# The sink columns of the probabilities: their high and low parts moved from VectorE to ScalarE and GpSimd

## The chip, the core and the metric

The kernel runs on one core of a Trainium2 chip. A core has TensorE (matrix products and transposes, into PSUM), VectorE, ScalarE and GpSimd (elementwise work; GpSimd has no way to PSUM in this kernel, all its operands are in SBUF), and queues that issue DMA transfers. Each engine works through its own instructions in order and waits for the others by semaphores. The metric is the device time of one execution in microseconds (us); lower is better.

## What is computed

Three parts follow each other: attention with a few sink columns and a sliding window, a mixture of experts with one expert for each token, and a second mixture in which all experts are used, weighted by a matrix that is normalized by rows and columns in turn. The change lies in the first part:

```python
B, H, S, D = q.shape                      # 2, 8, 768, 64; n_sink = 4, window = 128
scores = scale * np.matmul(q, k.transpose(0, 1, 3, 2))
keep = (pos[None, :] < n_sink) | ((rel >= 0) & (rel < window))   # rel = row - column
scores = np.where(keep, scores, -1e9)
a = np.exp(scores - scores.max(-1, keepdims=True))
a = a / (a.sum(-1, keepdims=True) + 1e-9)
return np.matmul(a, v)
```

## The kernel before

**Tiling.** Attention goes over 8 groups, each a pair of heads of one batch element, and in each group over 6 units t = 0 to 5 of 128 rows; 48 units in all. A row of unit t needs the 128 columns of its own tile, the 128 of the tile before and, from t = 2 on, the 4 sink columns, which lie apart from them. So a score tile is 128 x 260: the tile before, 4 sink columns, its own tile (128 x 128 for t = 0).

**A unit.** `st_a` makes one head's scores: a product on TensorE (L359), mask and minimum on VectorE (L360, from PSUM), the exponential on ScalarE (L362), giving `pt` in SBUF. The product with v is made in float16 in two parts, high and low. `st_b` transposes `pt` on TensorE (L370, `tq`), ScalarE makes the high part `ph` from it (L388), VectorE the low part `pl` (L398). The sink columns go another way. `psk_hi` (L378) writes their high part, scaled by 16384, twice into `psk`; `psk_lo` (L382) writes the low part behind it. `st_b3` transposes `psk` (24 columns: three parts, two heads, four sinks) in one step on TensorE (L393, `tk`), and ScalarE copies it (L395, `skT`). `st_c` multiplies with v: the sink part first (L410, against `vk`), then the rest (L416 to L419, against `vs`). `norm` divides by the row sums for two units at a time (L427 to L432). There are 32 units with t of 2 or more, so 32 of each of L378, L382, L393 and L395.

**The next group's operands** (`prep`) are spread over eight steps: the transposes of k and q (L236, copied out by L239, L246, L248), the largest |v| (L254 to L277), and on GpSimd the scaling of v (L284, in the fifth step of a group), its low part (L287, twice) and the sink values `vk` (L297 to L302, a chain of six small instructions in the second step of the next group).

**Order.** In step i the loop (L484 to L535) works on four units: scores of unit i + 2, `psk` of unit i + 1, transposes of unit i, product of unit i - 1. Inside the loop the order of ScalarE's and of GpSimd's instructions is the program's own (`manual_schedule`, L482); TensorE's and VectorE's order is set by a planner at build time, near the program's. `psk_hi` is called early in a step, ahead of `st_b2` (ScalarE's L388), and `psk_lo` between the two `st_a`. `pt` has four buffers, `psk` three, `tq`, `sc` and `tp` two.

**Beside it.** Routing (`route`, L779) is spread over the steps from the fifth group on: logits on TensorE, small VectorE instructions, then the scatter of the rows of the first batch element by GpSimd (L750, then L751, an indirect DMA whose descriptors GpSimd makes). Near the end, from step 43 (`SPLIT0`), the first expert's weights are split: high parts on ScalarE (L775), low parts on GpSimd for the first two and on VectorE for the others (L776); after each pair the next weights are loaded into the freed buffers.

Of the kernel before, what the change touches and what calls it, by code (L numbers as in the profile page):

```python
# [8 lines left out]
F32 = mybir.dt.float32  # L9
# [5 lines left out]
AF = mybir.ActivationFunctionType  # L15
ALU = mybir.AluOpType
# [4 lines left out]
P = 128  # L21
# [5 lines left out]
G = 2  # L27
NS = 4
# [9 lines left out]
PSC = 16384.0  # L38
# [121 lines left out]
def attention_fast(nc, tc, c, a, x_bs, hooks):  # L160
# [6 lines left out]
    wk = st.enter_context(tc.tile_pool(name="af_wk", bufs=3))  # L167
# [206 lines left out]
    def psk_hi(u):  # L374
        if u and u.t >= 2:
            u.psk = wk.tile([P, 3, G, NS], F16, name="psk")
            u.pk = u.pt[:, :, P:SB]
            nc.vector.tensor_scalar(u.psk[:, 0:2], u.pk.unsqueeze(1).broadcast_to([P, 2, G, NS]), PSC, None, ALU.mult)  # L378

    def psk_lo(u):  # L380
        if u and u.t >= 2:
            nc.vector.scalar_tensor_tensor(u.psk[:, 2], u.pk, PSC, u.psk[:, 0], ALU.mult, ALU.subtract)  # L382

    def v3(u, x):
        return x[:, :, 1, :] if u.t == 0 else x.rearrange("p h c q -> p (h c q)")
# [57 lines left out]
    for gi, (b, g) in enumerate(groups):  # L443
        for t in range(NT):
            u = Ctx()
# [31 lines left out]
    head_masks()  # L477
    r.v_s()
    psk_hi(units[0])
    psk_lo(units[0])  # L480
    ms.close()
    st.enter_context(tc.manual_schedule(engines={ENG.Activation, ENG.Pool}))  # L482
    ready = []
    for i in range(len(units) + 2):  # L484
# [10 lines left out]
        steps.run("act", *ready)  # L495
        norm(un, 0)
        psk_hi(up)
        norm(un, 1)
        run(m0)
# [17 lines left out]
        if ua:  # L517
            st_a(ua, 0)
        psk_lo(up)
        run(m1)  # L520
        steps.run("dve")
# [1150 lines left out]
```

## Time and profile before

| | |
|---|---|
| median of 3 runs | 1324.7 us (1322.53 to 1326.58) |
| profiled execution, in all | 1326.13 us |
| its span, first to last instruction | 1324.3 us |
| TensorE busy | 1272.4 us (96%) |
| VectorE busy | 969.9 us (73%) |
| ScalarE busy | 578.7 us (44%) |
| GpSimd busy | 449.3 us (34%) |
| mean granted TensorE clock | 0.986 |

The page of the profile shows one execution. Engines: PE is TensorE's products, PEld its weight loads, DVE VectorE, ACT ScalarE, POOL GpSimd, SP the queue that issues DMA transfers. L360 is line 360 of the kernel. Busy time counts the time from an instruction's start to its end, and the records of neighbours can overlap. Idle time before an instruction is put down to what came last, as `<-DVE psk L382`. The granted clock is the share of full speed that TensorE was given: 1.00 is 2.4 GHz, 0.50 is 1.2 GHz. Times of one instruction in a list of groups are means in ns. A row in order of time gives the start and the length in us; in the list by stage, a row gives the stretch, its length, and how long each engine was busy in it.

### The profile page before, as it was taken

The page shows a single profiled execution, that of the slowest core. Times are in us where ns is not written, and L with a number is a line of the kernel's source. Part 1 is how long each engine was busy: PE and PEld are TensorE (multiplying, and loading weights), DVE is VectorE, ACT ScalarE, POOL GpSimd, SP SyncE. Part 2 cuts the span into 40 slices and gives each one's busy share as a digit, 9 for nine tenths or more (in the row PEclk, how much of TensorE's full clock was granted, in tenths as well). Part 3 has the DMA queues.
Part 4 walks back from the last instruction along what each step waited for, and adds up shares of the span by engine and source line. Part 5 has one row for each costly group of instructions (what it writes and reads, how often), then busy time and mean ns, then how long its engine had stood idle before and what let it go on. Part 6 is the DMA issues. An engine that isn't in the chain of part 4 may idle for free.

```text
span 1324.3 us, 19440 instructions
## 1 busy us (share of the span) xinstructions
PE 1272.4 (96%) x7177; PEld 761.2 (57%) x7177; DVE 969.9 (73%) x2141; ACT 578.7 (44%) x1055; POOL 449.3 (34%) x438
## 2 busy tenths in 40 slices
PE   6999799889898999999999999999999999999998
PEld 4766589788744555555555555555555555555553
DVE  7979675455388877777777777777777777777765
ACT  4876534545363455434443343334334434443331
POOL 2326321262352323332243233223422332343223
PEclk9999899989999999999999999999999999999999
DMA  5424624552111111111121111112211111121002
GB/s 110 109 55 140 173 97 167 162 144 64 43 33 25 36 37 52 36 37 36 37 55 41 50 36 36 37 37 42 51 52 37 36 37 36 38 55 41 16 1 96
DMA packets 114306, 80.23 MB, mean 61 GB/s; under 512 B 50196, under 2 KB 97300, under 8 KB 114196
## 3 DMA queue, kind: packets, MB, share of 16 engines
q1 hardware_dynamic: 112276, 72.51, 21.7%
q0 software_dynamic: 1920, 6.32, 1.3%
q8 instruction: 61, 1.00, 0.3%
q14 instruction: 49, 0.40, 0.1%
HBM read 71.94 MB, written 6.87 MB: 60 GB/s over the span
## 4 chain that ended last, share of the span: by engine, by line
PE 64%; DVE 4%; issue 3%; ACT 1%; POOL 1%; POOLq 0%; ACTq 0%
PE y L1513 34%; PE bk L1459 30%; DVE hl L1468 1%; DVE cb L1471 1%; DVE xlo L1202 0%; ACT hh L1465 0%; POOL out_dram L1533 0%; DVE x L1526 0%; ACT w1h L1050 0%; DVE wmax L1010 0%; POOL w2l L1061 0%; DVE wsc L1021 0%; ACT x L1524 0%; ACT xhi L1199 0%; DVE pp L1442 0%
## 5 line engine op out<-in xcount | busy, mean ns | idle before, releaser
L1526 DVE SCALAR_TENSOR_TENSOR x<-y,pps,x 128x512 f32<-128x512 f32 x332 | 243.9, 748 | 115.4 <-PE y L1513 115.3
L1513 PE MATMUL y<-w2h,hh 128*128 128x512 f16 x768 | 291.6, 380 | 1.1 <-DVE x L1526 0.5
L1513 PE MATMUL y<-w2h,hl 128*128 128x512 f16 x768 | 291.8, 380 | 0.0
L1513 PE MATMUL y<-w2l,hh 128*128 128x512 f16 x768 | 291.8, 380 | 0.0
L1513 PEld LDWEIGHTS <-hh 128*128 128x128 f16 x1536 | 150.7, 98 | 175.2 <-issue 2.6
L1471 DVE SCALAR_TENSOR_TENSOR cb<-bk,cb 128x384 f32<-128x384 f32 x384 | 189.8, 550 | 81.9 <-PE bk L1459 81.9
L1459 PEld LDWEIGHTS <-w1h 128*128 128x128 f16 x1792 | 175.1, 98 | 128.5 <-issue 7.5
L1044 POOL TENSOR_TENSOR wsum<-raw2a 128x256 f32<-128x256 f32 x155 | 109.3, 740 | 295.8 <-issue 245.7
L1465 ACT ACTIVATE hh<-cb 128x384 f16<-128x384 f32 x256 | 126.4, 523 | 177.4 <-DVE cb L1471 177.4
L1473 ACT ACTIVATE cb<-bk 128x384 f32<-128x384 f32 x64 | 31.4, 490 | 296.8 <-PE bk L1459 296.2
L1055 POOL TENSOR_TENSOR w1l<-raw2a,w1h 128x256 f16<-128x256 f32 x64 | 51.4, 822 | 309.2 <-ACT w1h L1049 309.2
L1459 PE MATMUL bk<-x_b,w1h 128*128 128x384 f16 x448 | 146.6, 327 | 4.5 <-DVEq L1358 4.5
L1459 PE MATMUL bk<-xl,w1h 128*128 128x384 f16 x448 | 146.6, 327 | 0.0
L1459 PE MATMUL bk<-xhi,w1h 128*128 128x384 f16 x448 | 146.0, 326 | 0.5 <-ACT cb L1473 0.5
L1459 PE MATMUL bk<-x_b,w1l 128*128 128x384 f16 x448 | 146.5, 327 | 0.0
L1459 PE MATMUL bk<-xhi,w1l 128*128 128x384 f16 x448 | 146.0, 326 | 0.0
L1459 PE MATMUL bk<-xlo,w1h 128*128 128x384 f16 x448 | 146.0, 326 | 0.0
L1468 DVE SCALAR_TENSOR_TENSOR hl<-cb,hh 128x384 f16<-128x384 f32 x256 | 133.6, 563 | 9.3 <-ACT hh L1465 1.5
L1513 PEld LDWEIGHTS <-hl 128*128 128x128 f16 x768 | 75.2, 98 | 90.9 <-issue 0.6
L1459 PEld LDWEIGHTS <-w1l 128*128 128x128 f16 x896 | 87.8, 98 | 58.3 <-issue 0.5
L1056 POOL TENSOR_TENSOR w1l<-wsum,w1h 128x1280 f16<-128x1280 f32 x31 | 81.1, 2615 | 0.2 <-ACT w1h L1050 0.2
L1061 POOL TENSOR_TENSOR w2l<-raw2b,w2h 128x1024 f16<-128x1024 f32 x32 | 68.8, 2151 | 10.5 <-ACT w2h L1060 10.5
(369 smaller groups left out, 1939.7 us busy)
## 6 DMA issues: line engine op xcount, KB each, us to landing
raw2b<-in_moe_w_dram SPq DMA_DIRECT2D x40, 512.0 KB, 3.5
raw2a<-in_moe_w_dram SPq DMA_DIRECT2D x64, 256.0 KB, 3.1
r<-in_moe_w_dram SPq DMA_DIRECT2D x24, 512.0 KB, 6.7
raw2a<-in_moe_w_dram SPq DMA_DIRECT2D x8, 512.0 KB, 6.1
wall<-dmax SPq DMA_DIRECT2D x32, 128.0 KB, 4.4
xrow<-scr SPq DMA_DIRECT2D x4, 832.0 KB
raw_v<-in_v_dram SPq DMA_DIRECT2D x8, 384.0 KB, 3.9
raw_k<-in_k_dram SPq DMA_DIRECT2D x14, 192.0 KB, 3.0
```

The lines of the kernel that those rows point to most:

```text
L1044: nc.gpsimd.tensor_tensor(ws[:, s_], x, y, op)
L1055: nc.gpsimd.tensor_tensor(wl[:, 4 + i], w1_block(n, i, i), wh[:, 4 + i], ALU.subtract)
L1056: nc.gpsimd.tensor_tensor(wl[:, 0:5], ws, wh[:, 0:5], ALU.subtract)
L1061: nc.gpsimd.tensor_tensor(vl, raw2[n % 2][1], vh, ALU.subtract)
L1459: nc.tensor.matmul(bank, w[wi][:, WSLOT[m], k], X[xi][sb][m - 1][:, k], start=(first and i == 0), stop=(i == 5), skip_group_check=True)
L1465: nc.scalar.activation(h[0][:, i, l], cb[:, 2 * i + l], AF.Relu)
L1468: nc.vector.scalar_tensor_tensor(h[1][:, i, l], cb[:, 2 * i + l], 0.0, h[0][:, i, l], ALU.max, ALU.subtract)
L1471: nc.vector.scalar_tensor_tensor(x[0], bank, sign * HSC, x[1], ALU.mult, ALU.add)
L1473: nc.scalar.activation(c22, b0, AF.Copy, scale=HSC)
L1513: nc.tensor.matmul(y, h[hi_][:, i, l, t * P:(t + 1) * P], w[wi][:, i], start=(i == 0 and pi == 0), stop=(i == 1 and pi == 2))
L1526: nc.vector.scalar_tensor_tensor(dst, y, f if e == 0 else pps[n % 3][:, T:T + 1], acc, ALU.mult, ALU.add)
```

## The change

For the 32 units with sink columns, the high part of the sink columns is written by ScalarE, as a scaled copy. The scaled value itself, in float32, is written by GpSimd into a new tile `pks`, and the low part is a GpSimd subtraction of the two. Three instructions take the place of two, and VectorE has none of them. They are issued at the same places of a step. Nothing else is edited.

```diff
     def psk_hi(u):
         if u and u.t >= 2:
             u.psk = wk.tile([P, 3, G, NS], F16, name="psk")
             u.pk = u.pt[:, :, P:SB]
-            nc.vector.tensor_scalar(u.psk[:, 0:2], u.pk.unsqueeze(1).broadcast_to([P, 2, G, NS]), PSC, None, ALU.mult)
+            u.pks = wk.tile([P, G, NS], F32, name="pks")
+            nc.gpsimd.tensor_scalar(u.pks, u.pk, PSC, None, ALU.mult)
+            nc.scalar.activation(u.psk[:, 0:2], u.pk.unsqueeze(1).broadcast_to([P, 2, G, NS]), AF.Copy, scale=PSC)
 
     def psk_lo(u):
         if u and u.t >= 2:
-            nc.vector.scalar_tensor_tensor(u.psk[:, 2], u.pk, PSC, u.psk[:, 0], ALU.mult, ALU.subtract)
+            nc.gpsimd.tensor_tensor(u.psk[:, 2], u.pks, u.psk[:, 0], ALU.subtract)
```

## Rows read from the trace of the kernel before

**Rows 1.** us by stage: engine busy (instructions), granted clock, DMA share, GB/s
```profile
52.64:66.75 14.11, 14.11 (x137) 10.72 (x136) 13.79 (x58) 11.33 (x30) 5.22 (x10) 1.00 0.38 86
...
84.69:104.10 19.41, 19.41 (x175) 13.73 (x174) 15.96 (x76) 13.79 (x36) 5.24 (x10) 1.00 0.19 44
...
138.40:155.00 16.60, 12.56 (x116) 8.77 (x115) 16.07 (x42) 10.80 (x23) 6.28 (x8) 0.79 0.60 176
...
450.00:1300.00 850.00, 850.00 (x4549) 444.78 (x4548) 637.70 (x1215) 346.38 (x593) 279.69 (x256) 1.00 0.17 39
```

**Rows 2.** VectorE in order of time: start us, us, engine, line, operation
```profile
26.10 0.17 DVE L378 TENSOR_SCALAR psk<-pt 128x16 f16<-128x16 f32 x1
26.18 0.27 DVE L261 TENSOR_REDUCE vmm<-tp 1x1 f32<-1x128 f32 x1
...
26.73 0.15 DVE L382 SCALAR_TENSOR_TENSOR psk<-pt,psk 128x8 f16<-128x8 f32 x1
26.80 0.16 DVE L305 COPY kb<-kb 128x24 f32<-128x24 f32 x1
```

**Rows 3.** groups by line, 20 to 155 us: xcount | busy us, mean ns
```profile
L382 DVE SCALAR_TENSOR_TENSOR psk<-pt,psk 128x8 f16<-128x8 f32 x32 | 14.6, 455 | 0.1
...
L378 DVE TENSOR_SCALAR psk<-pt 128x16 f16<-128x16 f32 x32 | 9.5, 297 | 0.2 <-ACT pt L362 0.2
...
L267 DVE TENSOR_TENSOR vmm<-vmm,expm 1x1 int32<-1x1 int32 x7 | 2.2, 313 | 0.0
...
L305 DVE COPY kb<-kb 128x24 f32<-128x24 f32 x7 | 1.2, 173 | 0.0
```

**Rows 4.** VectorE in order of time, around the first long stall
```profile
31.14 0.29 DVE L360 CUSTOM_DVE_ANT_0 pt<-sc,mk 128x128 f32<-128x128 f32 x1
...
31.36 1.36 DVE L382 SCALAR_TENSOR_TENSOR psk<-pt,psk 128x8 f16<-128x8 f32 x1
```

**Rows 5.** GpSimd in order of time
```profile
31.23 1.47 POOL L284 TENSOR_TENSOR raw_v<-raw_v,vinv 128x768 f32<-128x768 f32 x1 [5.03 <-DVE vinv L277]
...
40.26 0.18 POOL L302 CAST vk<-hm 24x2 f16<-24x2 f32 x1
...
107.66 1.17 POOL L751 DMA_INDIRECT scr<-x_b,pos  x1 [0.29 <-POOL x_b L750]
...
140.27 2.35 POOL L776 TENSOR_TENSOR w1l<-r,w1h 128x1024 fp32r<-128x1024 f32 x1
```

**Rows 6.** VectorE in order of time, three more of the long stalls
```profile
108.20 1.74 DVE L382 SCALAR_TENSOR_TENSOR psk<-pt,psk 128x8 f16<-128x8 f32 x1
...
130.99 1.44 DVE L382 SCALAR_TENSOR_TENSOR psk<-pt,psk 128x8 f16<-128x8 f32 x1
...
140.66 4.28 DVE L378 TENSOR_SCALAR psk<-pt 128x16 f16<-128x16 f32 x1
```

**Rows 7.** TensorE in order of time, the transposes of psk
```profile
32.77 0.23 PE L393 MATMUL tk<-ident_h,psk 128*24 128x128 f16 x1
...
40.04 0.23 PE L393 MATMUL tk<-ident_h,psk 128*24 128x128 f16 x1
...
110.00 0.23 PE L393 MATMUL tk<-ident_h,psk 128*24 128x128 f16 x1 [1.96 <-DVE psk L382]
...
145.42 0.28 PE L393 MATMUL tk<-ident_h,psk 128*24 128x128 f16 x1 [3.43 <-DVE psk L382]
```

**Rows 8.** groups by line, 20 to 155 us: small GpSimd and ScalarE instructions
```profile
L298 POOL TENSOR_TENSOR vl<-vr,vh 24x64 f16<-24x64 f32 x8 | 2.4, 298 | 0.6
...
L302 POOL CAST vk<-hm 24x2 f16<-24x2 f32 x8 | 1.5, 186 | 0.0
...
L296 ACT ACTIVATE vh<-vr,vinv 24x64 f16<-24x64 f32 x8 | 2.7, 332 | 0.0
...
L835 ACT ACTIVATE rt<-rt 128x48 f32<-128x48 f32 x1 | 0.2, 226 | 0.0
```

**Rows 9.** one microsecond after a TensorE wait: columns as in rows 1
```profile
111.00:112.00 1.00, 1.00 (x3) 0.33 (x1) 0.97 (x6) 1.00 (x4) 0.11 (x1) 0.50 0.00 0
```

## The prediction

> **What bounds the kernel now.** I read the stages first [rows 1]. From 450 us on TensorE is busy throughout, so that two thirds of the span only shift with what comes earlier; nothing of the change lies there. The changed lines run in attention, 24 to 155 us. In a typical group of six units (14.11 us) VectorE is busy for 13.79 us, ScalarE for 11.33 and GpSimd for 5.22. TensorE shows 14.11, but its records overlap: every small matmul lasts some 0.2 us in the records although the next starts long before that. VectorE therefore bounds the ordinary group. The stage from 84.69 to 104.10 differs: VectorE is busy 15.96 of 19.41 us, since TensorE does the routing logits in between. In the last stage VectorE is busy again (16.07 of 16.60) while TensorE stands at 12.56 and its clock at 0.79.
>
> Next I asked what VectorE is busy with. The two lines that move away, L378 and L382, have 32 instructions each [rows 3], and their means (297 and 455 ns) are far above the ordinary ones of 0.17 and 0.15 us [rows 2]. The difference is stalls that count as busy. The total is 14.6 + 9.5 = 24.1 us; 32 x (0.17 + 0.15) = 10.2 us are ordinary, so 13.9 us are stalls. In order of time there are nine long ones. Seven are L382 beside the scaling of v (L284): the first takes 1.36 us and ends when the 1.47 us of L284 end [rows 4, 5], the last takes 1.44 [rows 6]. One takes 1.74 us beside the scatter, one of 4.28 us is L378 beside the weight splits of L776 [rows 5, 6]. L360, which reads PSUM, starts before L284 and keeps its 0.29 us while L284 runs [rows 4].
>
> **The change part by part.** *Slots removed.* The next instruction starts 0.08 us after L378 and 0.07 after L382 [rows 2], so a pair costs VectorE 0.15 us in sequence (the 0.32 of their durations overlap with the neighbours): 32 x 0.15 = 4.8 us. I leave out 7 pairs, in the stage of the logits and at the end, where VectorE does not bind: 25 x 0.15 = 3.8 us gained (bounds 0 and 4.8).
>
> *The seven stalls at L284.* They hold about 7 x 1.2 - 0.5 = 7.8 us of VectorE (13.9 less 4.1, 1.6 and some small ones). But the new subtraction is issued on GpSimd in program order, after L284 of the same step. L284 ends at 32.70 [rows 5]; with 0.2 to 0.3 us for a small GpSimd instruction [rows 8] psk is whole at 32.95, and the transpose that stands at 32.77 [rows 7] starts near 33.0. TensorE takes its work in order, so the scores behind it are no earlier than now, while VectorE arrives 1.2 us earlier and fills part of that with its other work. I take 0.8 of 1.2, in the six groups where VectorE binds: 4.8 us (bounds 0 and 7.8).
>
> *The stall at L776.* GpSimd gets the pair of one unit between its two L776. The first ends at 140.27 + 2.35 = 142.62 [rows 5]; two small instructions make 143.1, and the transpose follows at 143.2 in place of 145.42 [rows 7]: 2.2 us gained (bounds 0 and 4.1). The second L776 starts later by 0.5, and the next unit's pair stands behind it, near 145.8; that unit is ready only then anyway. This also covers the DMA loads that wait for the L776 buffers: 0.5 us later for one of four, with no reader before 155 us.
>
> *The stall at the scatter.* The pair of that unit is now queued behind the descriptor work of L751, which ends at 108.83 [rows 5]; psk is whole at 109.3 in place of 109.9, so the transpose of 110.00 [rows 7] comes 0.6 us earlier (bounds 0 and 1.6).
>
> *New wait: the pair behind the sink values.* In the second step of a group GpSimd builds vk (L297 to L302). The pair comes behind it. Its last instruction ends at 40.26 + 0.18 = 40.44 [rows 5], the pair at 40.9, but the transpose now runs at 40.04 [rows 7]. That is 0.9 us of waiting on TensorE, behind which the scores of a later unit, and on ScalarE the copy of tk and two exponentials, are queued. Scores are made ahead of use, so I charge about half: 7 x 0.4 = 2.8 us lost (bounds 0 and 6.3).
>
> *ScalarE.* 32 new instructions at 0.226 to 0.332 us [rows 8]; 0.23 is nearest by size, 7.4 us in all. Four in a group are 0.9 us against 14.11 - 11.33 = 2.8 idle [rows 1], so the ordinary group hides them. Where VectorE does not bind, in the same 7 units as above, they stand ahead of the copy of ph that others wait for: 7 x 0.23 = 1.6 us lost (bounds 0 and 7.4, the latter if nothing covers them).
>
> *GpSimd against VectorE.* The stalls above show that a VectorE instruction with two SBUF operands waits for a running GpSimd instruction. Of those that stay, L267 has one such stall in its 7 instructions (2.2 us in total), L305 none [rows 3]. With 64 short GpSimd instructions more, I charge 0.5 us (bounds 0 and 14 x 0.3 = 4.2).
>
> The Trainium skill ("SBUF - State Buffer", section "SBUF: two separate sides") says that VectorE, for an instruction with two SBUF inputs or in a two-port mode, and GpSimd lock one shared port pair for a whole instruction, and the loser blocks entirely. The stall that ends with L284 agrees [rows 4, 5]. By that rule each of the new GpSimd instructions is a holder too; if all 14 instructions of L267 and L305 met one, the sum below would be 4.2 - 0.5 = 3.7 us worse.
>
> *Sum.* 3.8 + 4.8 + 2.2 + 0.6 - 2.8 - 1.6 - 0.5 = 6.5 us. The profiled execution has a span of 1324.3 us and 1326.1 in all, 1.8 around the span; the sum gives it a span of 1317.8 and 1319.6 in all. The median of the runs shown, 1324.7, is 1.4 lower than the profiled one, so I forecast 1318.2. The pair itself is hidden as long as it ends before the next unit's transpose; without that cover, each late one costs what it is late.
>
> **The rivals.** *Everything comes back.* If neither queue holds the transposes, VectorE's whole 4.8 + 7.8 + 4.1 + 1.6 = 18.3 us are gained, less 1.6, 0.5 and 2.1 that the logits stage swallows: 14 us, 1311. For it: VectorE has almost no idle time in the ordinary group. Against: the transposes behind L284 and behind vk, whose rows leave no room.
>
> *The stall only changes its place.* The late pair takes what the removed stall gives. With vk at its bound (6.3), L284 at 0.3 in each of six groups (1.8) and the other terms as above: 3.8 + 1.8 + 2.2 + 0.6 - 6.3 - 1.6 - 0.5 = 0, so 1325. For it: psk is built one step ahead only, and GpSimd is in order. Against: 0.9 us of waiting on TensorE is less than the time by which its scores run ahead.
>
> *Slower, by TensorE's clock.* After the transpose at 110.00 had waited 1.96 us, the clock fell to 0.50, 1.2 GHz [rows 7, 9], and stayed there for some 3 us; work of that length at half the speed costs about 1.5 us. If the late pair behind vk makes TensorE idle as long as there, it pays this in all 7 groups. It decides where that wait, by my rows 0.9 us, reaches about 2. In all groups that is 10.5 us on top of the 1325, in four of them 6: 1331. Against: the wait is half as long as the one shown, and the waits of 1.96 and 3.43 us [rows 7], which now bring the clock down, get shorter.
>
> **How the numbers follow.** My forecast 0.52, everything back 0.12, stall moved 0.23, slower 0.13. The forecast's own range, with its terms off by a third each, is 1314 to 1322. Of its 0.52 some 0.07 lies above 1320.7, which is 0.3% (4 us) under the median and about what a measurement of this kernel can tell from no change. Faster is 0.45 + 0.12 = 0.57, within 0.3% 0.07 + 0.23 = 0.30, slower 0.13. The range from 1311 to 1327.5 takes in the case in which all comes back and the moved stall, and leaves out most of the slower one and a little below.
>
> **What would show it.** In the changed profile VectorE should have no L378 or L382 and no stall beside L284; its busy time between 20 and 155 us should fall by 15 us or more. The transposes of psk should wait for GpSimd, at about 0.2 us behind L284 and 0.4 to 0.9 behind vk. Units' exponentials should still wait for VectorE's minimum; if they wait for ScalarE's own new line, that term was too small. The last attention work should end near 149 us in place of 155, and everything from there on should be the same length. I am wrong if TensorE waits 2 us and more for GpSimd in every group, if another VectorE instruction takes over the stall at L284, or if the time gained by 155 us is spent again before 450.

## The result and the profile after

The change makes the kernel slower. The changed kernel takes 1334.9 us (median of 10 executions), the kernel before on the same chip 1326.9 (also 10), 7.9 us less. The ratio on record is 1.0065 with a 95% interval of 1.0048 to 1.0082, or 8.6 us; it and the ratios below are not quotients of two medians and differ from these by up to 0.001. In a later set of runs it came to 1.0062 (1.0039 to 1.0085). I had forecast 1318.2 and a range up to 1327.5.

The profiled execution of the changed kernel has a span of 1330.9 us, the one before 1324.3. The first instruction behind attention, an iota on GpSimd, starts at 162.22 us against 155.65: 6.6 us later, which is the whole difference of the spans. In these two executions, then, all of it arises in attention. (This profiled execution is one of the shorter ones, 1332.7 against the median of 1334.9.)

The busy time by stage in the changed kernel, to be read against [rows 1]; columns as there. The fourth row is one ordinary group, the fifth the stage of the weight splits:

```profile
24.00:28.00 4.00, 2.75 (x18) 1.49 (x15) 4.00 (x17) 1.35 (x5) 2.21 (x4) 1.00 0.56 135
28.00:32.00 4.00, 4.00 (x27) 2.80 (x27) 2.49 (x7) 3.09 (x10) 1.62 (x5) 0.52 0.02 4
32.00:36.00 4.00, 4.00 (x26) 3.02 (x25) 1.93 (x9) 1.86 (x6) 1.24 (x3) 0.63 0.06 15
63.56:79.13 15.57, 13.89 (x139) 11.02 (x139) 12.15 (x48) 11.95 (x32) 6.76 (x19) 1.00 0.35 78
138.26:155.00 16.74, 13.98 (x124) 10.08 (x123) 11.64 (x41) 13.72 (x33) 14.18 (x22) 0.88 0.48 136
450.00:1300.00 850.00, 849.27 (x4540) 444.01 (x4538) 641.58 (x1227) 346.10 (x592) 282.93 (x261) 1.00 0.18 39
```

VectorE did get free: 12.15 us in a group, where it had 13.79. But the group takes 15.57 us in place of 14.11. From 450 us on nothing has changed. And there is something new near the beginning: TensorE is thin from 24 to 28 us (2.75 of 4), and its clock is then at 0.52 and 0.63, which is partly at 1.2 GHz. In the kernel before, the clock stood at 1.00 there:

```profile
24.00:28.00 4.00, 3.24 (x27) 2.34 (x28) 3.97 (x27) 2.74 (x7) 1.34 (x4) 1.00 0.19 3
28.00:32.00 4.00, 4.00 (x43) 2.92 (x43) 3.91 (x18) 2.94 (x8) 0.77 (x1) 1.00 0.02 4
```

Who waits now, from the waits of the changed kernel, 20 to 163 us (engine and line, what it waited for: us in total, times, longest):

```profile
DVE pt L360 <- PE sc L359: 19.9, 27, 2.9
...
PEld L395 <- POOL psk L384: 15.7, 12, 2.4
...
PE tk L395 <- POOL psk L384: 12.5, 10, 2.2
ACT skT L397 <- PE tk L395: 8.4, 10, 2.6
```

In the kernel before, in the same view:

```profile
PE tk L393 <- DVE psk L382: 5.6, 3, 3.4
DVE pt L360 <- PE sc L359: 4.5, 8, 1.2
```

TensorE's transposes waited for `psk` at three places there, of which the two long ones stand in [rows 7]. The order of the engines has turned round: VectorE waits for TensorE's scores, and TensorE waits for GpSimd's low part. One such place, GpSimd in order of time, then TensorE, then VectorE:

```profile
57.28 0.18 POOL L302 CAST vk<-hm 24x2 f16<-24x2 f32 x1
57.43 0.23 POOL L379 TENSOR_SCALAR pks<-pt 128x8 f32<-128x8 f32 x1
57.74 0.20 POOL L384 TENSOR_TENSOR psk<-pks,psk 128x8 f16<-128x8 f32 x1
```

```profile
58.00 0.23 PE L395 MATMUL tk<-ident_h,psk 128*24 128x128 f16 x1 [1.68 <-POOL psk L384]
58.15 0.70 PE L359 MATMUL sc<-kb,qz 128*128 128x260 f32 x2
```

```profile
58.89 0.43 DVE L360 CUSTOM_DVE_ANT_0 pt<-sc,mk 128x260 f32<-128x260 f32 x1 [1.63 <-PE sc L359]
```

This is the chain I had called the new wait: `vk`, the pair, the transpose, the scores in TensorE's order behind it, and VectorE, idle for 1.63 us.

The pace of the groups can be read from the starts of L284, one in each group (GpSimd in order of time, changed kernel; the first row is the filling of `xrow` with zeros, of which more below):

```profile
23.73 1.81 POOL L664 MEMSET xrow<- 128x2048 f32 x1
...
31.14 1.47 POOL L284 TENSOR_TENSOR raw_v<-raw_v,vinv 128x768 f32<-128x768 f32 x1
...
48.00 1.47 POOL L284 TENSOR_TENSOR raw_v<-raw_v,vinv 128x768 f32<-128x768 f32 x1
...
63.56 1.47 POOL L284 TENSOR_TENSOR raw_v<-raw_v,vinv 128x768 f32<-128x768 f32 x1
...
79.13 1.47 POOL L284 TENSOR_TENSOR raw_v<-raw_v,vinv 128x768 f32<-128x768 f32 x1
...
101.65 1.47 POOL L284 TENSOR_TENSOR raw_v<-raw_v,vinv 128x768 f32<-128x768 f32 x1
```

The same in the kernel before, where the first starts at 31.23 [rows 5] and the fill at 10.46:

```profile
10.46 1.81 POOL L662 MEMSET xrow<- 128x2048 f32 x1
...
45.83 1.47 POOL L284 TENSOR_TENSOR raw_v<-raw_v,vinv 128x768 f32<-128x768 f32 x1 [5.32 <-DVE vinv L277]
...
59.93 1.47 POOL L284 TENSOR_TENSOR raw_v<-raw_v,vinv 128x768 f32<-128x768 f32 x1 [4.82 <-DVE vinv L277]
...
74.05 1.47 POOL L284 TENSOR_TENSOR raw_v<-raw_v,vinv 128x768 f32<-128x768 f32 x1 [4.82 <-DVE vinv L277]
...
96.21 1.47 POOL L284 TENSOR_TENSOR raw_v<-raw_v,vinv 128x768 f32<-128x768 f32 x1 [8.54 <-DVE vinv L277]
```

The distances are 16.9, 15.6, 15.6 and 22.5 us; in the kernel before 14.6, 14.1, 14.1 and 22.2. At the fourth L284 the changed kernel is 5.1 us behind. From there to the end of attention it takes 83.1 us against 81.6; runs below in which VectorE still makes `psk` take 80.7 to 84.1 (e12, e11), so nothing can be read from these 1.5 us.

### The profile page after: what moved, and what is told of

Its sections match the earlier page's. It is cut to its first block, busy times and chain, and to the rows that moved or that the text cites. A ratio compares the mean times of both kernels' runs of the same rounds, so it can differ in the third digit from the quotient of the medians.

```text
span 1330.9 us, 19493 instructions
## 1 busy us (share of the span) xinstructions
PE 1272.1 (96%) x7177; PEld 762.2 (57%) x7177; DVE 953.2 (72%) x2077; ACT 583.7 (44%) x1087; POOL 462.6 (35%) x502
## 4 chain that ended last, share of the span: by engine, by line
PE 65%; issue 3%; DVE 3%; ACT 1%; POOL 1%; POOLq 0%
PE y L1515 34%; PE bk L1461 30%; DVE cb L1473 1%; PE y L1226 0%; DVE x L1528 0%; POOL out_dram L1535 0%; DVE hl L1470 0%; ACT hh L1467 0%; DVE xlo L1204 0%; DVE wmax L1012 0%; POOL w2l L1063 0%; DVE wsc L1023 0%; ACT x L1526 0%; ACT xhi L1201 0%; DVE pp L1444 0%
## 5 line engine op out<-in xcount | busy, mean ns | idle before, releaser
L1461 PEld LDWEIGHTS <-w1l 128*128 128x128 f16 x896 | 87.8, 98 | 58.3 <-issue 0.5
```

Source lines behind the costliest of these rows:

```text
L1461: nc.tensor.matmul(bank, w[wi][:, WSLOT[m], k], X[xi][sb][m - 1][:, k], start=(first and i == 0), stop=(i == 5), skip_group_check=True)
```

## The experiments

Each ratio is against the kernel before, timed on the same chip; that one's medians were 1326.9 to 1331.2 us on the chips used. "Group" is the distance of the second to the third and of the third to the fourth L284 in the profiled execution.

| run | what runs | ratio, 95% interval | group, us |
|---|---|---|---|
| changed kernel | | 1.0065 (1.0048 to 1.0082) | 15.6, 15.6 |
| e15 | the same again | 1.0062 (1.0039 to 1.0085) | 15.6, 15.6 |
| e2 | high part alone moved | 1.0011 (0.9997 to 1.0024) | 13.7, 14.0 |
| e3 | low part alone moved | 1.0057 (1.0039 to 1.0074) | 14.9, 15.0 |
| e4 | moved instructions without a reader | 1.0029 (1.0013 to 1.0044) | 14.1, 14.1 |
| e1 | pair at the head of the step | 1.0031 (1.0018 to 1.0043) | 14.8, 15.1 |
| e8 | before, more TensorE work | 1.0039 (1.0025 to 1.0054) | 14.6, 15.0 |
| e7 | before, low part right behind the high one | 0.9999 (0.9984 to 1.0013) | 14.1, 14.1 |
| e5, e16 | changed, early fill | 1.0018 (1.0001 to 1.0034), 1.0042 (1.0027 to 1.0057) | 15.6, 15.6 |
| e6 | early fill, pair meant to go ahead of `vk` | 1.0018 (1.0003 to 1.0033) | 15.5, 16.0 |
| e11 | before, fill held up | 1.0015 (0.9999 to 1.0031) | 14.1, 14.1 |
| e9, e18 | early fill, `vk` behind the pair | 1.0022 (1.0008 to 1.0036), 1.0049 (1.0031 to 1.0067) | 14.5, 14.5 |
| e17 | `vk` behind the pair, fill held up | 1.0063 (1.0044 to 1.0083) | 14.5, 14.5 |
| e10 | as e9, last three groups on VectorE | 1.0032 (1.0020 to 1.0044) | 14.5, 14.5 |
| e12 | unread copies in the last three groups | 0.9997 (0.9982 to 1.0011) | 14.1, 14.1 |
| e13 | early fill, first five groups changed | 1.0049 (1.0034 to 1.0063) | 15.6, 15.6 |
| e14 | last three groups changed | 1.0017 (0.9998 to 1.0036) | 14.1, 14.1 |

Two rows of one kernel (e5 and e16, e9 and e18) stand 0.0024 and 0.0027 apart. They ran on different chips, so that some 3 us can hide between two chips, and no smaller difference across chips is read below. Side by side on one chip ran e1 to e4; e5 to e8; e9 and e10; e11 and e12; e13 to e16; e17 and e18.

### Which half of the change loses the time

**e2**, the kernel before with only the high part on ScalarE:

```diff
-            nc.vector.tensor_scalar(u.psk[:, 0:2], ..., PSC, None, ALU.mult)
+            nc.scalar.activation(u.psk[:, 0:2], ..., AF.Copy, scale=PSC)
```

> The kernel before with the high part alone moved to ScalarE; the low part stays on VectorE. Theory Q: no wait on GpSimd arises, so no slower than before; VectorE loses 32 x 0.08 = 2.6 us of slots and the 4.28 us stall of L378 moves to L382 or goes; 1323 to 1327. Theory S: most of the loss, 1332 to 1336. Theory L: as before, 1326.

**e3**, the changed kernel with the high part back on VectorE:

```diff
-            nc.scalar.activation(u.psk[:, 0:2], ..., AF.Copy, scale=PSC)
+            nc.vector.tensor_scalar(u.psk[:, 0:2], ..., PSC, None, ALU.mult)
```

> The changed kernel with the high part left on VectorE; the float32 product and the low part are on GpSimd at the places of the change. Theory Q: all of the loss, 1332 to 1337, with the same waits of 1.3 to 1.7 us at the transpose behind vk. Theory S: near 1326. Theory L: 1332 to 1337, but with VectorE stalled and not waiting for scores.

ScalarE's part costs nothing that can be measured and gains nothing: 1.0011. GpSimd's part alone loses nearly everything, 1.0057, and TensorE waits for it as in the changed kernel, though the ordinary group grows by 0.8 us here and not by 1.5. The waits of e3:

```profile
PEld L395 <- POOL psk L384: 14.5, 14, 2.8
...
PE tk L395 <- POOL psk L384: 11.1, 8, 2.6
```

e2 says something of the bound, too. It takes 32 instructions from VectorE, and the group moves from 14.1 to 14.0 and 13.7.

### Is it the reader that waits, or the work itself

**e1**, the changed kernel with both calls at the head of the step, ahead of the next group's work on GpSimd:

```diff
         ua, up, ub, uc, un = at(i + 2), at(i + 1), at(i), at(i - 1), at(i - 2)
+        psk_hi(up)
+        psk_lo(up)
         run(e)
...
-        psk_hi(up)
...
-        psk_lo(up)
```

> The changed kernel with psk_hi and psk_lo called at the head of a step, ahead of the sink values vk and of the other work that GpSimd gets in that step; the engines are those of the change. Theory Q (the change is slow because the low part stands behind vk, the weight splits and the scatter in GpSimd's queue, and TensorE waits for it in order): the waits of 1.3 to 1.7 us before the transpose of psk behind vk go, 7 x 1.5 = 10 us against the changed kernel, so 1323 to 1327, no longer than before. Theory S (ScalarE's 32 new instructions cost the time): still near 1335. Theory L (the short GpSimd instructions hold up VectorE): still near 1335. If VectorE alone bounds an ordinary group, all three parts of my forecast come back and it is 1316 to 1320; if TensorE is as full as VectorE, no less than 1322.

In e1 TensorE waits for the low part at two places in place of ten, 4.0 us in place of 12.5. But the low part of v (L287) now stands behind the pair in GpSimd's order, and TensorE waits 5.8 us for that at six places. The group falls to 14.8 and 15.1 us and the loss to 1.0031. So the time does not come back to that of the kernel before, as the theory of the wait had it: one wait is taken in part for another. The fill of `xrow` is held up in this run as well (24.15 us).

**e4**, the kernel before with the three moved instructions added, writing tiles that nobody reads:

```diff
+            u.pks = wk.tile([P, G, NS], F32, name="pks")
+            u.spare = wk.tile([P, 3, G, NS], F16, name="spare")
+            nc.gpsimd.tensor_scalar(u.pks, u.pk, PSC, None, ALU.mult)
+            nc.scalar.activation(u.spare[:, 0:2], ..., AF.Copy, scale=PSC)
...
+            nc.gpsimd.tensor_tensor(u.spare[:, 2], u.pks, u.spare[:, 0], ALU.subtract)
```

> The kernel before with the change's three instructions added in their places, writing spare tiles that nobody reads; VectorE still makes psk. Theory Q: no reader waits, so 1325 to 1329. Theory S: the 32 ScalarE instructions cost as in the changed kernel or more, 1333 to 1336. Theory L: the 64 GpSimd instructions do, 1333 to 1336, and VectorE's own psk instructions show more stall than the 13.9 us of before.

e4 was to cost nothing by the theory of the wait. It cost 1.0029, though its ordinary groups are the 14.1 us of the kernel before. So a second cause was there that needs no reader. The trace of e4 shows where: GpSimd in order of time, then two stretches with the columns of [rows 1].

```profile
23.00 1.81 POOL L667 MEMSET xrow<- 128x2048 f32 x1
...
29.04 1.47 POOL L284 TENSOR_TENSOR raw_v<-raw_v,vinv 128x768 f32<-128x768 f32 x1
...
47.35 1.47 POOL L284 TENSOR_TENSOR raw_v<-raw_v,vinv 128x768 f32<-128x768 f32 x1
```

```profile
28.00:32.00 4.00, 3.34 (x14) 1.91 (x13) 4.00 (x12) 2.85 (x8) 1.89 (x4) 0.66 0.24 53
32.00:36.00 4.00, 4.00 (x43) 2.89 (x43) 2.42 (x11) 1.61 (x5) 0.89 (x1) 0.50 0.39 115
```

The first distance is 18.3 us, 3.7 more than before, and the clock falls as in the changed kernel. The fill of `xrow` is issued in the third step of the loop. In the kernel before GpSimd had nothing ahead of it that waits for attention, so it ran at 10.46 us, out of everybody's way. Now new instructions stand ahead of it that wait for probabilities, and it runs at 23 us, in the middle of the first group.

What it does there is seen on VectorE of the changed kernel in order of time (it holds 23.73 to 25.54):

```profile
24.00 1.57 DVE L305 COPY kb<-kb 128x24 f32<-128x24 f32 x1
24.09 1.49 DVE L264 TENSOR_SCALAR vmm<-vmm 1x1 f32<-1x1 f32 x1
24.15 1.74 DVE L360 CUSTOM_DVE_ANT_0 pt<-sc,mk 128x260 f32<-128x260 f32 x1
```

L305 has a mean of 173 ns in [rows 3]; here it lasts until the fill ends. The Trainium skill ("SBUF — State Buffer", section "SBUF: two separate sides") says that a VectorE instruction in a two-port mode and a GpSimd instruction exclude each other on a shared port pair for a whole instruction. The row of L305 agrees, if that copy runs in such a mode, which no row tells.

### The fill

**e5** (repeated as **e16**), the changed kernel with the fill issued where the tile is made:

```diff
     def setup_a():
...
-        nc.gpsimd.memset(xrow, 0.0)
...
     xrow = rx.tile([P, 4, D], F32, name="xrow")
+    nc.gpsimd.memset(xrow, 0.0)
```

> The changed kernel, with one instruction moved: GpSimd's fill of xrow (1.81 us in both traces) is issued where the tile is made, ahead of attention. In the kernel before it ran at 10.46 us; in the changed one it stood behind the first probabilities in GpSimd's order and ran at 23.73, and TensorE's granted clock from 28 to 36 us was 0.52 and 0.63 there against 1.00. Theory C (the fill, held up by the new work, stalls VectorE, TensorE runs thin, and its clock falls): the clock is 1.00 from 24 to 40 us, the first L284 distance falls from 16.9 to about 15.6 as in the later groups, and the time falls by 2 to 4 us, to about 5 us over the kernel before. Theory Q (the wait behind the sink values alone): no change, 8 us over the kernel before.

> The changed kernel with the early fill once more, on the same chip as the changed kernel: 4 to 6 us under it if the fill and the clock that falls behind it are most of the loss; 2 us under it if the fill costs what it cost alone (1.0015), and then the two chips differed.

**e11**, the reverse: the kernel before, with two small GpSimd instructions that only hold the fill up:

```diff
+            if u.gi == 0 and u.t < 4:
+                spare = wk.tile([P, G, NS], F32, name="spare")
+                nc.gpsimd.tensor_scalar(spare, u.pk, PSC, None, ALU.mult)
```

> The kernel before and two 0.23-us GpSimd multiplications of the probabilities of units 2 and 3 into an unread tile, nothing else. They stand ahead of the fill of xrow in GpSimd's order, so that the fill (10.46 us in the kernel before) waits for these probabilities and runs at about 23 us, as in the changed kernel. Theory C (the held-up fill stalls VectorE there, TensorE runs thin, its clock falls): the fill starts at 22 to 24 us, the granted clock has a stretch near 0.5 between 26 and 38 us, and the time is 3 to 6 us over the kernel before, as the fifth run gave back some 6 of 8.6. If the fill is only a bystander: within 1 us.

With the early fill the first distance is 14.8 us in both runs, and the clock is 1.00 from 24 to 40 us. Three comparisons on one chip each bear on the price of the held-up fill: by the ratios e15 against e16 gives 2.7 us (1.0062 and 1.0042), e17 against e18 below 1.9 us (1.0063 and 1.0049), and e11 against the kernel before 2.0 us (1.0015). By the medians the three are 0.1, 0.9 and 1.9 us. None can be told from nothing, so by these the price lies between nothing and some 3 us. I had expected 4 to 6 from e5, on a chip on which the changed kernel did not run. In e11 the first distance is 16.4, though the clock stays at 1.00 there, so the stall can have a price of its own. But in e15 and e17 the fill is as late (22.85 and 23.21 us), and the first distance is 14.8 and 13.7, as in e16 and e18 with the early fill.

Whether the clock falls is not settled by the kernel alone. **e15** is the changed kernel itself:

> The changed kernel itself, beside the others: 6 to 10 us over the kernel before if its loss does not depend on the chip; 3 to 5 us if the first chip's was a large one.

Its rows for the first two of the stretches shown above:

```profile
24.00:28.00 4.00, 2.74 (x14) 1.49 (x13) 3.97 (x16) 2.02 (x6) 1.77 (x6) 1.00 0.56 135
28.00:32.00 4.00, 4.00 (x44) 3.13 (x43) 3.06 (x14) 3.33 (x12) 1.87 (x4) 1.00 0.01 4
```

TensorE is as thin as before the fall in the first trace (2.74 and 2.75 of 4), the fill ran at 22.85, and the clock stayed at 1.00; the first group took 14.8 us in place of 16.9. The Trainium skill ("TensorE: Matmul & The Clock Gate", section "Part 1: The HAM clock gate (the "warmup" mystery)") says of a kernel's first matmuls that their number at the lower clock differs from run to run; these two traces show such a difference in the middle of a kernel. This execution took 1331.7 us, the shortest of six on that chip. The time goes with the mean granted clock: three executions at 0.985 took 1331.7 to 1332.8 us, and three at 0.977 to 0.979 took 1337.6 to 1341.5.

### The pair behind the sink values

**e6** was to put the pair ahead of `vk` and did not: the step's list had one more entry behind `vk` than I had counted, so only the low part moved, to just behind the high one.

```diff
-        run(e)
+        run(e[:-1])
+        psk_hi(up)
+        psk_lo(up)
+        run(e[-1:])
```

> As the run before, and the pair of GpSimd instructions and ScalarE's high part are issued in the step's own list ahead of its last entry: ahead of the instructions that make vk, but behind the v low part (L287), on which the first trial of an earlier place had made TensorE wait (5.8 us over 6 places). If queue place and the held-up fill are all of the loss, the ordinary groups are 14.1 us again or less and the time is within 2 us of the kernel before. If VectorE alone had bounded the group, as the prediction had it, the time now comes out 5 us or more under the kernel before. If TensorE bounds it right under VectorE: 0 to 2 us under. If the pairs cost something by themselves that no place cures: 3 us or more over.

Its waits for `psk` are those of e5 (14.0 and 15.5 us on the weight load), and so is its time. It tells nothing of the place behind `vk`.

**e9** (repeated as **e18**) does it: the early fill, and `v_sink` is called behind the low part of the same step. **e17** is the same with the fill left where the change puts it.

```diff
-        e = [..., [L(v_lo, 1), v_sink]]
+        e = [..., [L(v_lo, 1)]]
+        r.v_s = v_sink
...
         psk_lo(up)
+        if i % NT == 1 and NT < i < len(units):
+            units[i].r.v_s()
```

> The changed kernel with the early fill, and the seven instructions that make vk (vh on ScalarE, six on GpSimd, about 2.2 us) are issued behind the low part of the same step instead of ahead of it. The run e6_order_and_zero was to do this and did not: the step's list has one entry more behind them, so the pair still stood behind vk. Theory Q (the pair's place behind vk costs the ordinary group its 1.5 us): TensorE's waits of 1.4 to 1.7 us for the low part go, the ordinary group falls from 15.6 to about 14 us, and the time is 5 to 8 us under the fifth run, 3 to 6 us under the kernel before. If TensorE holds the group as the run with more transposes says, 14 us is also the floor. If the waits only go to the next pair (the unit after), the group stays above 15 us and nothing is gained.

> The run e9_sink_behind_pair once more (1.0022 there): within 2 us of that, 1 to 5 us over the kernel before. If it comes out under the kernel before, the order alone was the loss and the change is worth something with it; if at 5 us or more over, the spread between chips is as large as what is looked for and the parts can't be told apart.

> The changed kernel with the instructions that make vk behind the pair, and the fill where the change leaves it. If the wait behind vk carries the loss: 0 to 4 us over the kernel before, an ordinary group of 14 to 14.6 us. If the fill carries it: 5 to 8 us over, with the first of the L284 distances 16 us or more. If both do, in parts: 3 to 6 us.

In the first groups the theory of the wait holds. TensorE's waits for the low part up to 95 us fall from 4.7 us (longest 1.7) to 1.8 (longest 0.6), and the group from 15.6 to 14.5. The fourth L284 starts at 71.89 in e9 and 72.81 in e17, against 75.1 to 75.7 in e5, e15 and e16, 79.13 in the first trace of the changed kernel and 74.05 in the kernel before. A group of 14.5 us is still 0.4 longer than before: the next unit's pair now stands behind `vk`, and TensorE waits 0.6 us for it in some groups. But the time gains nothing by it. From the fourth L284 to the end of attention e9, e18 and e17 take 88.8, 89.0 and 87.8 us, where the four executions of the changed kernel, with the fill early or not, take 82.7 to 87.2. The trace of e17 shows a wait that is new there. GpSimd, TensorE, and two stretches:

```profile
107.59 0.18 POOL L302 CAST vk<-hm 24x2 f16<-24x2 f32 x1
107.73 1.03 POOL L755 TENSOR_TENSOR x_b<-x_b,rs 128x512 f32<-128x512 f32 x1
109.06 1.20 POOL L756 DMA_INDIRECT scr<-x_b,pos  x1 [0.30 <-POOL x_b L755]
110.30 0.26 POOL L380 TENSOR_SCALAR pks<-pt 128x8 f32<-128x8 f32 x1
110.64 0.21 POOL L385 TENSOR_TENSOR psk<-pks,psk 128x8 f16<-128x8 f32 x1
```

```profile
110.90 0.23 PE L396 MATMUL tk<-ident_h,psk 128*24 128x128 f16 x1 [2.82 <-POOL psk L385]
```

```profile
108.00:112.00 4.00, 1.18 (x10) 0.63 (x10) 3.91 (x18) 2.04 (x6) 3.50 (x7) 1.00 0.18 67
112.00:116.00 4.00, 4.00 (x37) 3.13 (x35) 2.40 (x11) 2.08 (x6) 3.22 (x6) 0.55 0.89 237
```

`vk` now stands directly ahead of a scatter, and the next unit's pair behind both. TensorE waits 2.82 us for it here, and 2.48, 1.77 and 3.28 at three later places; where the changed kernel has such waits in this part, they are 0.4 to 2.2. Behind this one the clock falls to 0.55. What the first groups gain, the last ones lose. That these waits are the cause is not shown: in e10, below, VectorE makes `psk` in the last groups, and they are hardly shorter (87.9 us).

### Where in attention

In **e10** the last three groups of e9 are made by VectorE as in the kernel before; **e13** is e5 with the same exception; **e14** is the reverse, the first five groups on VectorE. The edit in e10 and e13 (in e14 with `u.gi < 5`):

```diff
+            if u.gi > 4:
+                nc.vector.tensor_scalar(u.psk[:, 0:2], ..., PSC, None, ALU.mult)
+                return
...
+        if u and u.t >= 2 and u.gi > 4:
+            nc.vector.scalar_tensor_tensor(u.psk[:, 2], u.pk, PSC, u.psk[:, 0], ALU.mult, ALU.subtract)
-        if u and u.t >= 2:
+        elif u and u.t >= 2:
```

**e12** is e4 with the same condition, so that it adds unread copies in the last three groups alone.

> The run e9_sink_behind_pair, and in the last three groups (those beside the scatters and the weight splits on GpSimd) both parts are made by VectorE as in the kernel before. Theory Q2 (in those groups the pairs stand behind scatters, a DMA wait of 3.4 to 3.8 us and two splits of 2.3 us, and the scatters behind the pairs): the stretch from the fifth of the seven multiplications L284 to the end of attention is 2 us or more shorter than in e9_sink_behind_pair, about 60 us as in the kernel before, and the time falls by as much. If that stretch is set by TensorE and its clock, no difference within 1.5 us.

> The kernel before, with the three new instructions of the change writing unread tiles as in the run e4_unread_copies, but in the last three groups alone, so that the fill is not held up. Theory Q2 (beside the scatters and splits the pairs hold GpSimd's queue up even without a reader): 1 to 3 us over the kernel before, and the seventh L284 distance 18 us or more against 16.0. If the 4 us of e4_unread_copies were the held-up fill alone: within 1 us of the kernel before.

> The changed kernel with the early fill, and the last three groups made by VectorE as in the kernel before: the new instructions stand in groups 0 to 4 alone, four of which showed 15.6 us for 14.1 with the fill out of the way. If the wait behind vk ends up in the time: 3 to 5 us over the kernel before. If the late stretch evens it out: within 1.5 us.

> The reverse: groups 0 to 4 made by VectorE as in the kernel before, the new instructions, with their reader, in the last three groups alone. The same without a reader cost nothing (0.9997). If TensorE waits there for a low part behind scatters and splits, as the rows of the changed kernel have it (0.4 to 2.2 us at six places): 2 to 5 us over the kernel before and six such waits in the trace. If these waits only take the place of waits that were there: within 1.5 us.

The first five groups alone lose 6.5 us (1.0049), with the fill out of the way; on the same chip the early fill with all groups changed loses 5.6 (e16). In the trace of e13 the four distances are 14.8, 15.6, 15.6 and 22.5 us, against 14.6, 14.1, 14.1 and 22.2 in the kernel before: together 3.5 us longer, nearly all of it in the second and third. So the wait behind `vk` lengthens the first groups by some 3.5 us; where the rest of the 6.5 lies the distances do not show. The last three groups alone lose 2.2, which cannot be told from nothing, with two waits for the low part (1.8 and 2.2 us) in place of the six that were expected; without a reader they lose nothing (0.9997). So the work on GpSimd as such costs at most 1.5 us beside the scatters (the interval of e12 ends at 1.0011), and the theory that the pairs hold the scatters up even without a reader is not borne out. e10 does not gain over e9: with `vk` moved, the last groups take long (87.9 us from the fourth L284) even where no pair is in them.

The parts do not add up to better than 3 us, since each execution also has its own falls of the clock in the last groups and behind attention. From the end of attention to the end of the span, where all kernels do the same work, the profiled executions take from 1168.5 us (e8) to 1176.6 (e18). These differences go with the granted clock in the first 300 us behind attention: in two halves it is 0.97 and 0.97 in the kernel before and in the changed kernel (1168.6 and 1168.7 us), 0.94 and 0.94 in e4 and e18 (1176.5 and 1176.6). What lets it fall in one execution and not in another, no run here tells.

### What bounds the ordinary group

**e8**, the kernel before with half of the transposes of the probabilities made twice into the same place:

```diff
-        for hh in range(G):
+        for hh in (0, 0, 1):
             for ci in u.cs:
                 nc.tensor.transpose(u.tq[:, hh, ci, :], ...)
```

> The kernel before with half of the fp32 transposes of the probabilities (L370) done twice into the same place: two more for each unit, 15 a group, starting about 0.11 us apart in the trace, so 1.65 us of TensorE a group and 13 us in all; no other engine gets any work. TensorE full under VectorE: 8 to 13 us slower, an ordinary group of 15.2 to 15.8 us. VectorE as the sole bound, with TensorE's 14.11 us of 14.11 only the overlap of records: 0 to 3 us.

The expectation counts 15 more transposes in a group; there are 11 (two for each of five units and one for t = 0), so the work added is 8 x 11 x 0.11 = 9.7 us and not 13. Of these the time takes up 5.2 us (1.0039). One ordinary group each of e8 and of e2, columns as in [rows 1]:

```profile
59.75:74.73 14.98, 14.98 (x149) 12.20 (x149) 13.55 (x57) 12.22 (x30) 5.20 (x10) 1.00 0.37 81
```

```profile
58.32:72.32 14.00, 13.99 (x138) 10.88 (x138) 13.49 (x52) 11.71 (x34) 5.21 (x10) 1.00 0.38 87
```

Work for TensorE alone lengthens the group although VectorE then has 1.4 us free: by 0.5 and 0.9 us of the 1.2 added. Work moved from VectorE to ScalarE shortens it by 0.1 to 0.4 us. So TensorE has no more than some 0.3 to 0.7 us of a group to spare in the kernel before (an estimate, by the 0.11 us for each transpose), and VectorE (13.79 of 14.11) about as little. Not excluded is that the added transposes lengthen the way from the scores to the product and not TensorE's own work; no run here tells these apart.

**e7** was to take the stall beside L284 away by calling the low part right behind the high one on VectorE.

```diff
         psk_hi(up)
+        psk_lo(up)
         norm(un, 1)
...
-        psk_lo(up)
```

> The kernel before with nothing on other engines: VectorE makes the low part right behind the high one, where GpSimd's 1.47-us multiplication has not begun. It takes only the stall of L382 away, some 1.2 us of VectorE in each of seven groups. VectorE as the sole bound: 5 to 8 us faster. TensorE bounding right under it: the ordinary group stays at 14 us and the time within 2 us. If the stall only goes to the next VectorE instruction: the same, and the rows of VectorE show a 1-us longer one at that place.

It does not decide anything, because the stall stayed. VectorE of e7 in order of time, beside an L284 that starts at 58.60:

```profile
58.95 1.14 DVE L382 SCALAR_TENSOR_TENSOR psk<-pt,psk 128x8 f16<-128x8 f32 x1
```

VectorE's order is not the program's, and the low part came to the same place. What VectorE's 1.2 us beside L284 are worth by themselves was therefore not measured. The changed kernel takes them away: L382's 1.3 to 1.4 us are gone there, and beside the first four L284 VectorE instead idles 0.6 to 0.8 us in front of L360, for TensorE's scores.

## Why the prediction was wrong

**What bounds the kernel.** Here the first step failed: "TensorE shows 14.11, but its records overlap ... VectorE therefore bounds the ordinary group." The records do overlap, but the reading that TensorE has room did not follow from that. The starts would have told: its transposes and scores follow each other without a gap, and no wait was shown on it in the group. e8 shows that work added to TensorE ends up in the time, in about half of its size. So the terms for the slots (3.8 us) and for the stalls (4.8) did not come: TensorE had only a few tenths of a microsecond of a group to spare. Without these two terms my sum is not 6.5 us gained but 2.1 lost. VectorE did save: its busy time from 24 to 162 us, where attention ends in the changed kernel, fell from 122.29 to 104.26, more than the 15 I had named as the sign. The saving became idle time in front of L360 (19.9 us for TensorE's scores, against 4.5).

**The wait behind the sink values.** The mechanism was right, and its size was wrong twice. I read the transpose's place in the first group, 40.04 [rows 7], which is 8.81 us behind L284 at 31.23 [rows 5]. In the later groups it stands at 53.97, 8.14 behind 45.83. In the changed kernel it is at 58.00, 10.00 behind 48.00, and at 73.57, 10.01 behind 63.56. So the delay is 1.86 us and not 0.9. I then charged half of it, since scores are made ahead of use; the ordinary group grew by 1.45, three quarters of it. But only two distances grew by so much, the first (with the early fill) by 0.2 and the fourth by 0.4: 3.5 us in four, against 1.6 for four in my sum. The run e9 shows that the order is the cause in the first groups: 14.5 us when `vk` stands behind the pair.

**The queue I did not look at.** I followed what the pair is queued behind, but not what is queued behind the pair. GpSimd had been free to run ahead; with 64 instructions that wait for probabilities its whole order is tied to attention's pace. The fill moved from 10.46 to 23.73 us, a cost that no term of my sum had, and my 0.5 us for GpSimd against VectorE counted short instructions only. I had also read from the stalls that VectorE instructions with two operands in SBUF are held; L378, held for 4.28 us [rows 6], has one, and so has L305, which the fill held.

**The splits and the scatters.** The pair did come between the two splits, as I had said, with its low part done at 150.2. The transpose waited 2.21 us there and 0.54 at the next unit, against 3.43 [rows 7]. From the last L284 to the end of attention it is 24.0 us against 24.7: 0.7 gained of the 2.2. At the scatter a wait of 1.96 us [rows 7] became two, 1.45 and 1.09, in place of one that is 0.6 shorter. The last distance between two L284, in which scatters lie, grew from 16.0 to 18.6; but it is 18.1 and 18.2 in e7 and e11 too, where VectorE makes `psk`, so the change is not shown to be the cause.

**ScalarE.** My 1.6 us are inside what e2 leaves open (1.0011, its interval ends at 1.0024, or 3.2 us). Its instruction takes 203 ns in the median, so 0.23 was about right. GpSimd's take 0.23 and 0.20, as estimated; the size of the moved work was never the problem.

**The rivals.** "The stall only changes its place" is what the ordinary group shows, with a late pair that takes more than the stall gave. "Slower, by TensorE's clock" named what did come true in the first trace, but at other places: I had tied it to the wait behind `vk` reaching 2 us in every group. Those waits are 1.3 to 1.7 us long, and the clock stays at 1.00 from 40 to 146 us in that trace. It fell behind the held-up fill, and behind the waits among scatters and splits (0.78 from 146 to 155 us). That it falls in one execution and not in another goes along with executions of this kernel lying 10 us apart.

**What the 8.6 us are made of.** The runs side by side on one chip give 5.6 to 6.5 us for the change with the fill out of the way (e16, e13), nearly all of it in the first five groups, and nothing to 3 us for the held-up fill. Some 3.5 us are the longer distances of the first groups. A part of the rest goes with the clock, whose mean is on record for each execution. The 17 of the kernel before beside e13 to e16 have 0.9844 on average, and among them 0.001 less clock goes with 0.9 us more time; e13, e15 and e16 have 0.9815 to 0.9818. By that, as an estimate, 2 to 2.5 us of their loss come with the lower clock, about a third. In e17 and e18, with `vk` behind the pair, the clock is 0.977 against 0.984, and by the executions on their own chip this makes some 5 us, about two thirds of their loss. So the edit that takes the wait behind `vk` away shortened the first groups by some 1.1 us each, and what was gained there is lost again beside a lower clock. Whether the waits among the scatters lower it, or something else, stays open, and so does the price of the wait behind `vk` alone. No arrangement that was run is measurably faster than the kernel before.

## What to carry to other kernels

Before work is moved off a full engine, ask what the next full engine is, and test it by adding work there: an engine whose records cover the whole group is not free because some of them overlap. When work goes to an engine that works through its queue in order and had run ahead, list what is queued behind the new instructions as well as ahead of them, since everything behind them now waits for their inputs. And take a slack in a repeating group from several of its repetitions, not from the first.

## What was not expected of the hardware

A fill of 1.81 us on GpSimd, which reads nothing, held VectorE until it ended: L305, a copy with a single input in SBUF, lasted from 24.00 to 25.57 us; whether L264 and L360 were held too or only stood behind it, the rows do not tell. Beside L284, which starts after it, L360 had kept its 0.29 us [rows 4]. The clock fell or stayed behind nearly equal stretches of TensorE work (2.75 and 2.74 of 4 us busy) in two executions of one kernel, and the first group took 16.9 us in the one and 14.8 in the other. A GpSimd instruction on 128 x 8 elements costs 0.20 to 0.23 us (medians), about as much as ScalarE's on 128 x 16 (0.20).
